# Decode attention on one core: the keys of a pair of units in one load, softmax parts of 160 and 96 tiles

## The chip, the cores and the metric

The kernel runs on one core of one Trainium2 chip. The metric is the device time of the execution in microseconds (us). A core has a TensorE (PE, matmul), a VectorE (DVE), a ScalarE (ACT), a GpSimd (POOL) and a SyncE (SP), and sixteen DMA engines that its queues share; SP's queue carries all loads of keys and values.

## The reference

Attention of one query position over 65,536 keys: 32 query heads of 128 elements, and 8 heads of keys and values, so that four query heads share one head of keys and values. All inputs are bfloat16.

```python
B, Hq, Hkv, Sq, Sk, D = 1, 32, 8, 1, 65536, 128

def reference(q, k, v):
    ...
    k = jnp.repeat(k, rep, axis=1)
    v = jnp.repeat(v, rep, axis=1)
    scale = D ** -0.5
    scores = jnp.einsum("bhqd,bhkd->bhqk", q, k) * scale
    p = _softmax(scores, axis=-1)
    return jnp.einsum("bhqk,bhkd->bhqd", p, v)
```

Keys and values are 134 MB each and are read once: 268.44 MB in all.

## The kernel before

**Work.** A head's 65,536 keys are four *units* of 16,384 (`HU = 4`); a unit is 128 *tiles* (`T`) of 128 keys. Two units of a head are a *pair*; there are 16 pairs (0 to 15), two for each head. In a pair, partition p holds 256 successive rows of keys (64 KB), and a tile is one row of each partition.

**Loads.** SP issues them in order. The keys of a pair come in two loads of 4 MB (128 partitions, 32 KB each) into `kbuf0` and `kbuf1`, one for each unit; the values of the pair come in one load of 8 MB (64 KB each partition) into `vbuf`. Before a key load SP waits for `kfree` of its buffer, before a value load for `vfree`. The first and the last loads are in pieces, so that work can start early and little is left behind the last one: the last unit's values come in pieces of 64, 32, 16, 10, 4 and 2 tiles (`V_PIECES`).

**One unit.** PE transposes tiles (by a matmul with the identity, line 125) in 16 groups of eight, into one of four PSUM banks `trb`; DVE (line 209) copies three of four groups to `ktb` in SBUF, ACT (line 207) the fourth (`on_act`). Then PE multiplies each transposed tile by the four queries `qcur` (line 136) into `qkb` of the unit, three groups (`LAG`) behind the transposes. When all scores of a unit are there, DVE takes their maximum for each partition (line 236), POOL the maximum over partitions (line 389), DVE combines it with the running maximum and gives the negative to ACT (lines 243 to 248), and ACT computes `alpha`, by which earlier sums are scaled (line 348), and four exponentials, one for each query, with their sums (line 352). An evicted group 15 gives the key buffer free (`kfree`, in `evict`, as soon as its transposes are done).

**A pair.** PE runs the keys of both units, then the values of both (line 155, 128 matmuls each, accumulated in `pvb`). DVE adds them to `acc` (lines 263, 269, 271) and only then increments `vfree`. The loop on PE is over pairs; DVE's is over heads, with both pairs written out.

**Order on the engines.** Each engine runs its instructions in the order written. `dve_round` and `act_round` fix by hand where the softmax steps stand between evictions; a wait (`take`) holds everything behind it on its engine. `pe_last` replaces the last value stage: it consumes the pieces as they land, and then the last result is transposed, scaled and stored by SP (line 440).

Of the kernel before, what the change touches and what calls it, by code (L numbers as in the profile page):

```python
# [22 lines left out]

LOOP_SLOT = 176


def on_act(j):
    return j % 4 == 3
# [14 lines left out]
def bass_standalone__gqa_softmax__decode_kernel(nc, q, k, v, out):  # L43
# [5 lines left out]
    assert D == P and Sk == P * T * HU and T * R == 512 and H >= 3 and NU % 2 == 0  # L49
# [27 lines left out]
    cmax = sb("cmax", [P, R], DT.float32)  # L77
# [5 lines left out]
    rsum = sb("rsum", [P, R], DT.float32)  # L83
# [12 lines left out]
    qkb = [S(nc.psum_tensor(f"qkb{i}", [P, T * R], DT.float32)) for i in range(2)]  # L96
    pvb = [S(nc.psum_tensor(f"pvb{i}", [P, 512], DT.float32)) for i in range(2)]
    fin = pvb[NU % 2]

    krdy = [sem(f"krdy{i}") for i in range(2)]  # L100
    khalf = [sem(f"khalf{i}") for i in range(2)]
    vrdy = [sem(f"vrdy{i}") for i in range(2)]
    vpiece = [sem(f"vpiece{i}") for i in range(len(V_PIECES))]
    kfree = [sem(f"kfree{i}") for i in range(2)]
    vfree = sem("vfree")
# [11 lines left out]
    def pe_transposes(pe, b, j):  # L117
        kv = kbuf[b][:, :].rearrange("p (t d) -> p t d", d=D)
        for i in range(TB):
            t = j * TB + i  # L120
            if t == 0:
                take(pe, krdy[b], 16)
            if t == HALF:
                take(pe, khalf[b], 16)
            ins = pe.transpose(trb[j % NTB][:, i * P:(i + 1) * P], kv[:, t, :], ident[:, :])  # L125
        ins.then_inc(tra if on_act(j) else trd, 1)

    def pe_scores(pe, b, j):
        done, (k, last) = eva if on_act(j) else evd, turn(j)
        if j == 0:  # L130
            take(pe, qrdy)
        if last:
            take(pe, done, k)
        for i in range(TB):
            t, off = j * TB + i, (j % NKG * TB + i) * P
            ins = pe.matmul(qkb[b][:, t * R:(t + 1) * R], lhsT=ktb[:, off:off + P],  # L136
                            rhs=qcur[:, :], start=True, stop=True)
            if i == 0 and not last:
                ins.wait_op(done, k, "sem-ge")
        if j == G - 1:  # L140
            ins.then_inc(qkd, 1)

    def pe_keys(pe, b):
        pend = []
        for j in range(G):
            pe_transposes(pe, b, j)
            pend.append(j)
            if len(pend) > LAG:
                pe_scores(pe, b, pend.pop(0))
        while pend:  # L150
            pe_scores(pe, b, pend.pop(0))

    def value(pe, b, t, first, last):
        vv = vbuf[:, :].rearrange("p (t d) -> p t d", d=D)
        return pe.matmul(pvb[b][:, 0:R], lhsT=vv[:, b * T + t, :], rhs=pts[b][:, t * R:(t + 1) * R],  # L155
                         start=t == first, stop=t == last)

    def pe_values(pe, b):
        take(pe, vrdy[b], 16)
        take(pe, exd)  # L160
        for t in range(T):
            ins = value(pe, b, t, 0, T - 1)
        ins.then_inc(pvd, 1)

    def pe_last(pe):
        b = (NU - 1) % 2
        starts = [sum(V_PIECES[:i]) for i in range(len(V_PIECES))]
        pe.wait_ge(t_o, H - 1)
        pe.transpose(qkb[0][0:HR - R, 0:P], oT[:, R:HR], identf[:, :]).then_inc(s_o, 1)
        take(pe, exd)  # L170
        for t in range(T):
            if t == starts[1]:
# [3 lines left out]
            ins = value(pe, b, t, 0, T - 1)  # L176
            if t in starts:
                ins.wait_op(vpiece[starts.index(t)], 16, "sem-ge")
# [5 lines left out]
    def tensor_engine(pe):  # L184
# [5 lines left out]
        with pe.Fori(0, NR) as i:  # L190
            pe_keys(pe, 0)
            pe_keys(pe, 1)
            pe_values(pe, 0)
            with pe.If(i < NR - 1):
                pe_values(pe, 1)
# [3 lines left out]
    def evict(e, n, j):  # L199
        dst = ktb[:, j % NKG * TB * P:(j % NKG + 1) * TB * P]  # L200
        k, last = turn(j)
        if last:
            take(e, tra if on_act(j) else trd, k)
        if j == G - 1:
            e.sem_inc(kfree[n % 2], 1)
# [4 lines left out]
        if not last:  # L210
            ins.wait_op(tra if on_act(j) else trd, k, "sem-ge")
# [10 lines left out]
    PART = [[j for j in range(a, b) if not on_act(j)] for a, b in ((0, 4), (4, 12), (12, G))]  # L222

    def evictions(e, n, parts):
        for part in parts:
            for j in part:
                evict(e, n, j)

    def scores_done(e, u):

        take(e, qkd)
        if u % HU == HU - 1:
            next_queries(e, qrdy)
        else:
            e.sem_inc(qrdy, 1)
        e.tensor_reduce(cmax[:, :], qkb[u % 2][:, :].rearrange("p (t g) -> p g t", g=R),  # L236
                        AX.X, ALU.max).then_inc(cm, 1)
# [12 lines left out]
    def add_sums(e, u):  # L250

        take(e, sx)
        if u % HU == 0:
            own(e, e.tensor_copy(lp[:, :], rsum[:, :]), xd)
        else:
            own(e, e.tensor_tensor(lp[:, :], lp[:, :], alpha[u % 2][:, :], ALU.mult), xd)  # L256
            own(e, e.tensor_tensor(lp[:, :], lp[:, :], rsum[:, :], ALU.add), xd)  # L257
# [7 lines left out]
    def add_values(e, u):  # L265
        take(e, pvd)
        pv = pvb[u % 2][:, 0:R]
        if u % HU == 0:
            own(e, e.tensor_copy(acc, pv), xd)  # L269
        else:  # L270
            own(e, e.tensor_tensor(acc, acc, pv, ALU.add), xd)  # L271

    def dve_round(e, i, h):

        a, b = 2 * i, 2 * i + 1
        evictions(e, a, PART)
        scores_done(e, a)
        evictions(e, b, PART[:1])
        maximum(e, a)
        evictions(e, b, PART[1:2])  # L280
        add_sums(e, a)
        evictions(e, b, PART[2:])
        scores_done(e, b)
        maximum(e, b)
        add_sums(e, b)
        rescale(e, a)
        add_values(e, a)
        rescale(e, b)
        if i < HALVES - 1:
            values_done(e, b)  # L290
        else:
            with e.If(h < H - 1):
                values_done(e, b)
                next_output(e)

    def values_done(e, u):
        add_values(e, u)
        e.sem_inc(vfree, 1)
# [23 lines left out]
    def vector_engine(e):  # L322
# [7 lines left out]
        with e.Fori(0, H) as h:  # L330
            for i in range(HALVES):
                dve_round(e, i, h)
        e.sem_inc(t_lp, 1)
        e.wait_ge(s_o, 1)
# [3 lines left out]
        ins = e.tensor_tensor(acc, acc, pvb[(NU - 1) % 2][:, 0:R], ALU.add)  # L338
# [6 lines left out]
    def exponentials(e, u):  # L345

        take(e, ng)
        e.activation(alpha[u % 2][:, :], dm[:, :], AF.Exp, scale=scale)  # L348
        sv = qkb[u % 2][:, :].rearrange("p (t g) -> p g t", g=R)
        pv = pts[u % 2][:, :].rearrange("p (t g) -> p g t", g=R)  # L350
        for g in range(R):
            ins = e.activation(pv[:, g, :], sv[:, g, :], AF.Exp, bias=negm[:, g:g + 1],  # L352
                               scale=scale, accum_out=rsum[:, g:g + 1])
# [4 lines left out]
    def act_round(e):  # L358
        for j in (3, 7, 11, 15):
            evict(e, 0, j)  # L360
        evict(e, 1, 3)
        exponentials(e, 0)
        for j in (7, 11, 15):
            evict(e, 1, j)
        exponentials(e, 1)

    def scalar_engine(e):
# [3 lines left out]
        with e.Fori(0, NR):  # L371
            act_round(e)
# [106 lines left out]
```

## Time and profile before

| | |
|---|---|
| median of 3 runs | 630.5 us (630.48 to 630.57) |
| the profiled execution | 630.56 us, span 628.5 us |
| PE busy | 489.2 us (78%) |
| DVE busy | 312.5 us (50%) |
| ACT busy | 186.6 us (30%) |
| POOL busy | 16.4 us (3%) |
| HBM read | 268.44 MB, 427 GB/s over the span |
| mean granted TensorE clock | 0.79 |

The span runs from the first to the last instruction of the profiled execution. PE's busy time is that of pipelined matmuls; PEld is its weight load, which overlaps. Rows of a timeline give the start and the duration in us, the engine, the line of the kernel and the operation. DMA rows of SP are issues; the transfer itself lands later.

### The profile page before, as it was taken

Reading aid. Unit: us, or ns where it says so; the run is one execution under the profiler, and the core shown is the slowest. Engines: PE = TensorE matmul, PEld = TensorE weight load, DVE = VectorE, ACT = ScalarE, POOL = GpSimd, SP = SyncE. Lnnn points to the kernel's source line nnn. Section 1 sums busy time; section 2 is a strip of 40 time slices with the busy share of each in tenths; the row PEclk is TensorE's granted clock in tenths of the full one; section 3 lists DMA queues with packets and bytes.
Section 4 is the critical chain, followed back from the end, with each engine's and each line's share of the span. In section 5 each row is a group of like instructions: output and inputs, shape, how many; then the busy total and the mean of one; then the engine's idle time right before and its main releaser. Section 6 shows DMA issues by size and latency. Waiting matters only on the chain. (4 is left out here: it accounts for less than half of the span.)

```text
span 628.5 us, 27046 instructions
## 1 busy us (share of the span) xinstructions
PE 489.2 (78%) x12293; PEld 482.3 (77%) x12293; DVE 312.5 (50%) x693; ACT 186.6 (30%) x418; POOL 16.4 (3%) x50
## 2 busy tenths in 40 slices
PE   4868859788696877967779686895868949689897
PEld 4758859687696877967679686895868949689896
DVE  4534726447273462725627256371563716537373
ACT  2321413314142141422414224041241413414141
POOL 0000000000000000000000000000000000000000
PEclk9776958769597695967959689696886969869596
DMA  8999999999999999999999999999999999999996
GB/s 369 439 426 446 434 415 453 415 453 430 419 448 419 448 419 434 453 413 455 407 432 438 425 438 430 430 455 409 455 413 438 442 415 448 417 434 432 423 444 283
DMA packets 8458, 268.58 MB, mean 427 GB/s; under 512 B 1026, under 2 KB 1282, under 8 KB 1538
## 3 DMA queue, kind: packets, MB, share of 16 engines
q1 hardware_dynamic: 8360, 268.44, 99.2%
q8 instruction: 7, 0.11, 0.1%
q10 hardware_dynamic: 90, 0.02, 0.0%
q14 instruction: 1, 0.01, 0.0%
HBM read 268.44 MB, written 0.01 MB: 427 GB/s over the span
## 5 line engine op out<-in xcount | busy, mean ns | idle before, releaser
L125 PE MATMUL trb<-ident,kbuf 128*128 128x128 bf16 x4096 | 328.3, 233 | 42.7 <-PEq L40 42.7
L209 DVE COPY ktb<-trb 128x1024 bf16<-128x1024 bf16 x384 | 254.2, 689 | 100.8 <-PE trb L125 97.5
L125 PEld LDWEIGHTS trb<-ident,kbuf 128*128 128x128 bf16 x4096 | 262.8, 105 | 43.7 <-issue 43.7
L207 ACT ACTIVATE ktb<-trb 128x1024 bf16<-128x1024 bf16 x128 | 131.1, 1024 | 379.1 <-PE trb L125 320.0
L136 PE MATMUL qkb<-qcur,ktb 128*128 128x4 bf16 x4096 | 170.9, 165 | 21.9 <-PEq L40 21.9
L136 PEld LDWEIGHTS qkb<-qcur,ktb 128*128 128x128 bf16 x4096 | 153.3, 97 | 26.0 <-issue 23.9
L155 PE MATMUL pvb<-pts,vbuf 128*128 128x4 bf16 x4096 | 112.3, 166 | 68.7 <-PEq L40 57.9
L155 PEld LDWEIGHTS pvb<-pts,vbuf 128*128 128x128 bf16 x4096 | 111.1, 104 | 70.1 <-issue 68.5
L352 ACT ACTIVATE pts<-qkb,negm 128x128 bf16<-128x128 f32 x128 | 50.5, 540 | 0.0
L236 DVE TENSOR_REDUCE cmax<-qkb 128x4 f32<-128x512 f32 x32 | 22.1, 692 | 43.2 <-DVEq L40 42.0
L271 DVE TENSOR_TENSOR acc<-acc,pvb 128x4 f32<-128x4 f32 x23 | 3.6, 158 | 62.8 <-DVEq L40 62.8
L352 ACT ACTIVATION_READ_ACCUMULATOR pts<-qkb,negm 128x1 f32 x128 | 34.6, 270 | 0.0
L389 POOL PARTITION_ALL_REDUCE cmaxa<-cmax x32 | 11.9, 372 | 576.3 <-POOLq L40 576.3
L348 ACT ACTIVATE alpha<-dm 128x4 f32<-128x4 f32 x32 | 6.6, 205 | 54.2 <-ACTq L40 53.4
L256 DVE TENSOR_TENSOR lp<-lp,alpha 128x4 f32<-128x4 f32 x24 | 3.8, 160 | 34.2 <-DVEq L40 34.2
L269 DVE COPY acc<-pvb 128x4 f32<-128x4 f32 x8 | 1.3, 162 | 25.5 <-DVEq L40 25.5
L246 DVE TENSOR_TENSOR m<-m,cmaxa 128x4 f32<-128x4 f32 x24 | 3.8, 159 | 11.5 <-DVEq L40 11.5
L218 DVE COPY qcur<-qT 128x4 bf16<-128x4 bf16 x9 | 1.5, 169 | 13.4 <-DVEq L40 13.3
L263 DVE TENSOR_TENSOR acc<-acc,alpha 128x4 f32<-128x4 f32 x24 | 3.9, 163 | 4.3 <-DVEq L40 1.9
L247 DVE TENSOR_TENSOR dm<-m 128x4 f32<-128x4 f32 x24 | 3.9, 162 | 3.5
L257 DVE TENSOR_TENSOR lp<-lp,rsum 128x4 f32<-128x4 f32 x24 | 3.9, 162 | 3.5
L391 POOL PARTITION_ALL_REDUCE la<-lp x8 | 3.4, 431 | 29.3 <-POOLq L40 29.3
(42 smaller groups left out, 23.7 us busy)
## 6 DMA issues: line engine op xcount, KB each, us to landing
kbuf<-in_k_dram SPq DMA_DIRECT2D x29, 4096.0 KB, 26.0
kbuf<-in_k_dram SPq DMA_DIRECT2D x6, 2048.0 KB, 21.1
vbuf<-in_v_dram SPq DMA_DIRECT2D x3, 4096.0 KB, 24.9
vbuf<-in_v_dram SPq DMA_DIRECT2D x1, 2048.0 KB, 29.4
vbuf<-in_v_dram SPq DMA_DIRECT2D x1, 1024.0 KB, 31.4
vbuf<-in_v_dram SPq DMA_DIRECT2D x1, 512.0 KB, 32.2
vbuf<-in_v_dram SPq DMA_DIRECT2D x1, 320.0 KB, 32.5
vbuf<-in_v_dram SPq DMA_DIRECT2D x14, 30.9
```

Of the source, the lines that this page charges most:

```text
L125: ins = pe.transpose(trb[j % NTB][:, i * P:(i + 1) * P], kv[:, t, :], ident[:, :])
L136: ins = pe.matmul(qkb[b][:, t * R:(t + 1) * R], lhsT=ktb[:, off:off + P], rhs=qcur[:, :], start=True, stop=True)
L155: return pe.matmul(pvb[b][:, 0:R], lhsT=vv[:, b * T + t, :], rhs=pts[b][:, t * R:(t + 1) * R], start=t == first, stop=t == last)
L207: ins = e.activation(dst, trb[j % NTB][:, :], AF.Copy).then_inc(eva, 1)
L209: ins = e.tensor_copy(dst, trb[j % NTB][:, :]).then_inc(evd, 1)
L236: e.tensor_reduce(cmax[:, :], qkb[u % 2][:, :].rearrange("p (t g) -> p g t", g=R), AX.X, ALU.max).then_inc(cm, 1)
L247: e.tensor_tensor(dm[:, :], mo[:, :], mn[:, :], ALU.subtract)
L257: own(e, e.tensor_tensor(lp[:, :], lp[:, :], rsum[:, :], ALU.add), xd)
L263: own(e, e.tensor_tensor(acc, acc, alpha[u % 2][:, :], ALU.mult), xd)
L348: e.activation(alpha[u % 2][:, :], dm[:, :], AF.Exp, scale=scale)
L352: ins = e.activation(pv[:, g, :], sv[:, g, :], AF.Exp, bias=negm[:, g:g + 1], scale=scale, accum_out=rsum[:, g:g + 1])
L389: e.partition_all_reduce(cmaxa[:, :], cmax[:, :], P, bass.bass_isa.ReduceOp.max).then_inc(cma, 1)
```

## The change

The keys of a pair are one load of 8 MB, with 64 KB for each partition, as the values are. `kbuf` is one buffer of 352 tiles: an even pair lies in tiles 96 to 351, an odd one in 0 to 255. Every pair's first 160 tiles (20 groups, `A`, `GA`) lie in tiles 96 to 255 of the buffer; the other 96 (`C`) lie behind them in an even pair and ahead of them in an odd one (`row_tile` maps a position to the row). So the next pair's keys may be loaded once group 19 is transposed. PE's code has the last 96 transposes twice, in two `If` blocks, for the two places.

The softmax runs over parts of 160 and 96 tiles. The first part's scores fill one PSUM bank and a quarter of a second, so it has two reductions and eight exponentials; the second part has one and four. PE scores the first 160 tiles three groups behind their transposes, then transposes all of the last 96, then scores these. DVE copies 23 of the 32 groups of a pair, ACT nine (24 and eight before); ACT's copies all stand ahead of its exponentials.

PE's value stage takes 64 tiles after the first part, 192 after the second, into three places of one bank. `vfree` is incremented when these matmuls are done, ahead of the additions. The last pair but one has keys and values in two loads each; the last has keys in three, and values in two and then pieces of 48, 24, 12, 6, 4 and 2 tiles.

Of the functions, the diff shows the lines of the new kernel, added and kept; the removed ones stand in the functions above.

```diff
@@ -9,23 +9,28 @@
 AX = mybir.AxisListType
 P = 128
 T = 128
+C = 96
+A = 2 * T - C
+K_PARTS = (0, 64, A)
 TB = 8
-G = T // TB
+G = 2 * T // TB
+GA = A // TB
+BANK = 512
 NTB = 4
-NKG = 8
+NKG = C // TB
 LAG = 3
 HU = 4
-HALF = T // 2
-V_PIECES = (64, 32, 16, 10, 4, 2)
-LOOP_SLOT = 176
+V_PIECES = (48, 24, 12, 6, 4, 2)
+LOOP_SLOT = 0
 def on_act(j):
-    return j % 4 == 3
+    return j % 4 == 2 if j < GA else (j - GA) % 3 == 1
...
+    def row_tile(odd, x):
+        return (x + C) % (2 * T) if odd else x
...
         return S(nc.semaphore(name))
-    kbuf = [sb(f"kbuf{i}", [P, T * D], DT.bfloat16) for i in range(2)]
+    kbuf = sb("kbuf", [P, (2 * T + C) * D], DT.bfloat16)
     vbuf = sb("vbuf", [P, 2 * T * D], DT.bfloat16)
     ktb = sb("ktb", [P, NKG * TB * P], DT.bfloat16)
-    pts = [sb(f"pts{i}", [P, T * R], DT.bfloat16) for i in range(2)]
+    pts = sb("pts", [P, 2 * T * R], DT.bfloat16)
     qsb = sb("qsb", [HR, D], DT.bfloat16)
     qT = sb("qT", [P, HR], DT.bfloat16)
...
@@ -114,68 +125,89 @@
+    def pe_transposes(pe, j, first):
+        for n, x in enumerate(K_PARTS):
+            if j == (x // TB if x < A else GA - 1):
+                take(pe, krdy[n], 16)
         for i in range(TB):
+            t = first + i
+            ins = pe.transpose(trb[j % NTB][:, i * P:(i + 1) * P], kbuf[:, t * D:(t + 1) * D],
+                               ident[:, :])
+            if i == 0 and j >= GA + NTB:
+                ins.wait_op(eva if on_act(j - NTB) else evd, turn(j - NTB)[0], "sem-ge")
         ins.then_inc(tra if on_act(j) else trd, 1)
+    def scores(x):
+        b = 2 if x >= A else x // T
+        return qkb[b], x - (0, T, A)[b]
+    def pe_scores(pe, j):
         done, (k, last) = eva if on_act(j) else evd, turn(j)
         if j == 0:
             take(pe, qrdy)
         if last:
             take(pe, done, k)
         for i in range(TB):
+            (bank, t), off = scores(j * TB + i), (j % NKG * TB + i) * P
+            ins = pe.matmul(bank[:, t * R:(t + 1) * R], lhsT=ktb[:, off:off + P],
                             rhs=qcur[:, :], start=True, stop=True)
             if i == 0 and not last:
                 ins.wait_op(done, k, "sem-ge")
+        if j in (T // TB - 1, GA - 1, G - 1):
             ins.then_inc(qkd, 1)
...
+    def pe_keys(pe, i):
+        for j in range(GA + LAG):
+            if j < GA:
+                pe_transposes(pe, j, C + j * TB)
+            if j >= LAG:
+                pe_scores(pe, j - LAG)
+        with pe.If(i % 2 < 1):
+            for j in range(GA, G):
+                pe_transposes(pe, j, C + j * TB)
+        with pe.If(i % 2 > 0):
+            for j in range(GA, G):
+                pe_transposes(pe, j, j * TB - A)
+        for j in range(GA, G):
+            pe_scores(pe, j)
+    def value(pe, out, r, first, last):
+        return pe.matmul(out, lhsT=vbuf[:, r * D:(r + 1) * D], rhs=pts[:, r * R:(r + 1) * R],
+                         start=first, stop=last)
+    def pe_values(pe):
+        for q, (a, b) in ((1, (C, A)), (0, (0, C)), (2, (A, 2 * T))):
+            if q in (1, 2):
+                take(pe, vrdy[q - 1], 16)
+            if q in (1, 0):
+                take(pe, exd)
+            for r in range(a, b):
+                ins = value(pe, pvb[:, q * R:(q + 1) * R], r, r == a, r == b - 1)
+        ins.then_inc(pvd, 1)
...
+    def pe_last(pe):
+        starts = [sum(V_PIECES[:i]) for i in range(len(V_PIECES))]
         take(pe, exd)
         pe.wait_ge(t_o, H - 1)
         pe.transpose(qkb[0][0:HR - R, 0:P], oT[:, R:HR], identf[:, :]).then_inc(s_o, 1)
+        for x in range(A):
+            ins = value(pe, pvb[:, 0:R], row_tile(True, x), x == 0, x == A - 1)
+            if x in (0, C):
+                ins.wait_op(vrdy[x // C], 16, "sem-ge")
+        ins.then_inc(pvd, 1)
         take(pe, exd)
+        for r in range(C):
+            if r == starts[1]:
                 pe.wait_ge(t_lp, 1)
                 pe.matmul(fin[0:R, P:P + 1], lhsT=lp[:, :], rhs=ones[:, :],
                           start=True, stop=True).then_inc(s_l, 1)
+            ins = value(pe, pvl[:, 0:R], r, r == 0, r == C - 1)
+            if r in starts:
+                ins.wait_op(vpiece[starts.index(r)], 16, "sem-ge")
         ins.then_inc(pvd, 1)
         ins = pe.transpose(fin[0:R, 0:P], acc, identf[:, :])
         ins.wait_op(t_acc, 1, "sem-ge")
...
+    def evict(e, j):
         dst = ktb[:, j % NKG * TB * P:(j % NKG + 1) * TB * P]
+        (k, last), done = turn(j), tra if on_act(j) else trd
         if last:
+            take(e, done, k)
+        if j == GA - 1:
+            e.wait_ge(done, k)
+            e.sem_inc(kfree, 1)
         if on_act(j):
             ins = e.activation(dst, trb[j % NTB][:, :], AF.Copy).then_inc(eva, 1)
         else:
             ins = e.tensor_copy(dst, trb[j % NTB][:, :]).then_inc(evd, 1)
+        if not last and j != GA - 1:
+            ins.wait_op(done, k, "sem-ge")
...
+    def evictions(e, a, b):
+        for j in range(a, b):
+            if not on_act(j):
+                evict(e, j)
+    def largest(e, b, n, to):
         take(e, qkd)
+        return e.tensor_reduce(to[:, :], qkb[b][:, 0:n * R].rearrange("p (t g) -> p g t", g=R),
+                               AX.X, ALU.max)
+    def first_part_done(e):
+        largest(e, 0, T, cmax[0])
+        own(e, largest(e, 1, A - T, cmax[1]), xd)
+        e.tensor_tensor(cmax[0][:, :], cmax[0][:, :], cmax[1][:, :], ALU.max).then_inc(cm, 1)
+    def pair_done(e, i):
+        if i == HALVES - 1:
             next_queries(e, qrdy)
         else:
             e.sem_inc(qrdy, 1)
...
+    def add(e, pv):
+        own(e, e.tensor_tensor(acc, acc, pv, ALU.add), xd)
+    def add_values(e, i):
+        rescale(e, 2 * i)
         take(e, pvd)
+        e.sem_inc(vfree, 1)
+        for n, q in enumerate((1, 2, 0) if i else (0, 1, 2)):
+            pv = pvb[:, q * R:(q + 1) * R]
+            if n == 2:
+                rescale(e, 2 * i + 1)
+            if i == 0 and n == 0:
+                own(e, e.tensor_copy(acc, pv), xd)
+            else:
+                add(e, pv)
...
     def dve_round(e, i, h):
         a, b = 2 * i, 2 * i + 1
+        evictions(e, 0, GA)
+        first_part_done(e)
+        evictions(e, GA, G - NTB)
         maximum(e, a)
+        evictions(e, G - NTB, G)
         add_sums(e, a)
+        largest(e, 2, C, cmax[0]).then_inc(cm, 1)
+        pair_done(e, i)
         maximum(e, b)
         add_sums(e, b)
         if i < HALVES - 1:
+            add_values(e, i)
         else:
             with e.If(h < H - 1):
+                add_values(e, i)
                 next_output(e)
...
@@ -344,32 +389,36 @@
     def exponentials(e, u):
         take(e, ng)
         e.activation(alpha[u % 2][:, :], dm[:, :], AF.Exp, scale=scale)
+        pv = pts[:, :].rearrange("p (t g) -> p g t", g=R)
+        for x, n, sums in ((A, C, 0),) if u % 2 else ((0, T, 0), (T, A - T, 1)):
+            bank, t = scores(x)
+            sv = bank[:, :].rearrange("p (t g) -> p g t", g=R)
+            r = row_tile(u // 2, x)
+            for g in range(R):
+                ins = e.activation(pv[:, g, r:r + n], sv[:, g, t:t + n], AF.Exp,
+                                   bias=negm[:, g:g + 1], scale=scale,
+                                   accum_out=rsum[sums][:, g:g + 1])
         own(e, ins, xa)
         e.sem_inc(exd, 1)
         e.sem_inc(sx, 1)
+    def act_round(e, i):
+        for j in range(G):
+            if on_act(j):
+                evict(e, j)
+        exponentials(e, 2 * i)
+        exponentials(e, 2 * i + 1)
...
     def sync_engine(e):
+        kp, vp = pairs(kf), pairs(vf)
+        def cols(a, b):
+            return slice(a * D, b * D)
+        def load_k(i, odd, split=(0,)):
+            for n, f in enumerate(split):
+                last = (split + (len(K_PARTS),))[n + 1]
+                a, b = K_PARTS[f], (K_PARTS + (2 * T,))[last]
+                r = row_tile(odd, a) if b - a < 2 * T else 0
+                t = r if odd else C + r
+                e.dma_start(kbuf[:, cols(t, t + b - a)], kp[i][:, cols(r, r + b - a)]).then_inc(krdy[f], 16)
+                for x in range(f + 1, last):
+                    e.sem_inc(krdy[x], 16)
+        def load_v(i, ready, a, b):
+            e.dma_start(vbuf[:, cols(a, b)], vp[i][:, cols(a, b)]).then_inc(ready, 16)
+        def load_both(i, odd):
+            take(e, kfree)
+            load_k(i, odd)
+            take(e, vfree)
+            load_v(i, vrdy[0], 0, 2 * T)
             e.sem_inc(vrdy[1], 16)
+        load_k(0, 0, (0, 1, 2))
+        load_v(0, vrdy[0], 0, 2 * T)
+        e.sem_inc(vrdy[1], 16)
+        load_both(1, 1)
+        with e.Fori(1, H - 1) as h:
+            load_both(2 * h, 0)
+            load_both(2 * h + 1, 1)
         i = NR - 2
+        take(e, kfree)
+        load_k(i, 0, (0, 2))
         take(e, vfree)
+        load_v(i, vrdy[0], 0, A)
+        load_v(i, vrdy[1], A, 2 * T)
         i = NR - 1
+        take(e, kfree)
+        load_k(i, 1, (0, 1, 2))
         take(e, vfree)
+        load_v(i, vrdy[0], C, 2 * C)
+        load_v(i, vrdy[1], 2 * C, 2 * T)
+        r = 0
+        for n, sm in zip(V_PIECES, vpiece):
+            load_v(i, sm, r, r + n)
+            r += n
         ins = e.dma_start(of[HR - R:HR, :], olast[:, :])
         ins.wait_op(t_last, 1, "sem-ge")
         ins.then_inc(o_sem, 16)
```

More of the change, by code (lines that the diff above doesn't have):

```diff
@@ L76, in bass_standalone__gqa_softmax__decode_kernel @@
     ones = sb("ones", [P, 1], DT.float32)
-    cmax = sb("cmax", [P, R], DT.float32)
+    cmax = [sb(f"cmax{i}", [P, R], DT.float32) for i in range(2)]
     cmaxa = sb("cmaxa", [P, R], DT.float32)
@@ L139, in pe_scores @@
                 ins.wait_op(done, k, "sem-ge")
-        if j == G - 1:
+        if j in (T // TB - 1, GA - 1, G - 1):
             ins.then_inc(qkd, 1)
[L143 to L156, printed above, removed]
@@ L332, in vector_engine @@
                 dve_round(e, i, h)
+        rescale(e, NU - 2)
+        take(e, pvd)
+        add(e, pvb[:, 0:R])
         e.sem_inc(t_lp, 1)
+        rescale(e, NU - 1)
         e.wait_ge(s_o, 1)
@@ L337, in vector_engine @@
         own(e, e.reciprocal(rl[:, :], fin[0:R, P:P + 1]), xd)
[L338 removed]
+        ins = e.tensor_tensor(acc, acc, pvl[:, 0:R], ALU.add)
         ins.wait_op(pvd, 1, "sem-ge")
@@ L370, in scalar_engine @@
         e.activation(dscr[:, 1:2], dscr[:, 0:1], AF.Exp, scale=1.0)
-        with e.Fori(0, NR):
-            act_round(e)
+        with e.Fori(0, H):
+            for i in range(HALVES):
+                act_round(e, i)
         e.wait_ge(t_row, 1)
```

135 lines of the change are left out of this document (15 added, 120 removed).

## The prediction

> **What bounds the kernel now.** I read the page first: the busy tenths of the DMA engines in 40 slices, the DMA queues and the issues.
>
> ```profile
> span 628.5 us, 27046 instructions
> DMA  8999999999999999999999999999999999999996
> q1 hardware_dynamic: 8360, 268.44, 99.2%
> q8 instruction: 7, 0.11, 0.1%
> qsb<-in_q_dram ACTq DMA_DIRECT2D x1, 8.0 KB, 2.2
> ```
>
> The load queue takes 99.2% of sixteen engines' span, and no slice between the first and the last is under nine tenths. So the kernel is bound by its loads, end to end. Then the DMA queue's own timeline, for one steady pair, and the landing times that go with it (the middle one of fourteen value loads; the two key loads of 491.63):
>
> ```profile
> 477.85 0.33 SPq L417 DMA_DIRECT2D vbuf<-in_v_dram  x1
> 491.63 11.61 SPq L413 DMA_DIRECT2D kbuf<-in_k_dram  x2
> 516.63 0.33 SPq L417 DMA_DIRECT2D vbuf<-in_v_dram  x1
> vbuf<-in_v_dram SPq DMA_DIRECT2D x14, 30.9
> DMA to landing us min/median/max: 25.3/26.1/26.9
> ```
>
> The value loads are issued 516.63 - 477.85 = 38.78 us apart: this is the period of a pair (8 MB of keys, 8 MB of values). Values land at 477.85 + 30.9 = 508.75; the second key load, issued at 491.63 + 11.61 - 0.33 = 502.91, lands 25.3 later, at 528.2; the next values at 547.5. So the key pair takes 19.45 and the values 19.3 (each to 0.1), and every load is issued long before the queue reaches it.
>
> The end is the third view, the chain in order of time, with the sizes and landings of the last pieces:
>
> ```profile
> 590.83 0.33 SPq L438
> ...
> 591.20 0.43 SPq L403
> ...
> 591.67 0.43 SPq L403
> ...
> 592.15 0.43 SPq L403
> ...
> 592.62 32.54 DMA vbuf<-in_v_dram
> ...
> 625.21 0.75 PE pvb L155 x16
> vbuf<-in_v_dram SPq DMA_DIRECT2D x3, 4096.0 KB, 24.9
> vbuf<-in_v_dram SPq DMA_DIRECT2D x1, 2048.0 KB, 29.4
> vbuf<-in_v_dram SPq DMA_DIRECT2D x1, 1024.0 KB, 31.4
> vbuf<-in_v_dram SPq DMA_DIRECT2D x1, 512.0 KB, 32.2
> vbuf<-in_v_dram SPq DMA_DIRECT2D x1, 64.0 KB, 32.1
> ```
>
> The last piece is issued at 593.57 (two steps of 0.475 after 592.62) and lands at 625.7; the last value matmul ends at 625.21 + 0.75 = 625.96, and 628.5 - 625.96 = 2.54 us of fixed tail follow. The profiled execution took 630.56 us, 2.06 more than its span; the median of the runs is 630.5, so I count from 630.5 and treat changes of the span as changes of the time.
>
> **Part 1, keys in one load.** The pieces price a load of 128 rows. 2 MB land at 591.20 + 29.4 = 620.6, the 1 MB after it at 623.07, the 0.5 MB at 624.35; the 4 MB before land at 590.83 + 24.9 = 615.73. Steps 4.87, 2.47, 1.28: halving the size leaves 2 x 2.47 - 4.87 = 0.07 and 2 x 1.28 - 2.47 = 0.09 us that don't halve. So each load costs some 0.08 us beside its bytes. Thirteen of the pairs 0 to 15 (1 to 13) go from two key loads to one; the last pair's keys from four to three and its values from seven to eight. Saved: 13 x 0.08 = 1.0 us. The bounds are nothing, and 13 x 0.15 = 2.0 by the 19.45 against 19.3 above; I take 1.0, from the pieces, whose steps are the cleaner. It lies on the path as long as the queue never runs dry and the loads still end last. By that the time would be 629.5.
>
> **Part 2, does the queue run dry?** Now keys of a pair arrive as a whole, so PE starts about 10 us later relative to the stream, and both buffers come free later. I build the new pair from the last pair of before, which starts right after a value stage as the new one's last pairs do:
>
> ```profile
> 591.45 3.57 PE L125 MATMUL trb<-ident,kbuf 128*128 128x128 bf16 x32 [1.17 <-PEq L40]
> 594.81 0.40 PE L136 MATMUL qkb<-qcur,ktb 128*128 128x4 bf16 x8
> 601.39 2.10 DVE L209 COPY ktb<-trb 128x1024 bf16<-128x1024 bf16 x3 [0.60 <-PE trb L125]
> 602.04 0.61 PE L125 MATMUL trb<-ident,kbuf 128*128 128x128 bf16 x8
> 602.68 0.61 PE L125 MATMUL trb<-ident,kbuf 128*128 128x128 bf16 x8
> 603.13 0.84 PE L136 MATMUL qkb<-qcur,ktb 128*128 128x4 bf16 x24
> 603.48 1.02 ACT L207 ACTIVATE ktb<-trb 128x1024 bf16<-128x1024 bf16 x1 [1.72 <-ACTq L40]
> 604.65 0.34 PE L136 MATMUL qkb<-qcur,ktb 128*128 128x4 bf16 x8 [0.68 <-PEq L40]
> 604.85 1.95 PE L125 MATMUL trb<-ident,kbuf 128*128 128x128 bf16 x32
> 606.64 0.34 PE L136 MATMUL qkb<-qcur,ktb 128*128 128x4 bf16 x8
> ```
>
> From the first transpose, s: sixteen groups of eight are transposed by 603.13 - 591.45 = 11.7; four more at 602.68 - 602.04 = 0.64 end at 14.3, and with that the new kfree is due (DVE group 19 waits for the transposes only). Draining the scores takes 604.99 - 603.13 = 1.86 in before, behind an ACT eviction of 1.02; now a DVE copy of 0.70 stands there: 1.54, so the first 160 tiles are scored at 15.8. The other twelve groups are transposed at (606.64 - 604.85) / 4 = 0.45 each: 21.2. DVE puts the two reductions between (below) and then eight copies of 0.70, about 22.5 at the end, just beside PE; I charge nothing, and up to 1 us if it is late. Their 96 scores at 0.84 / 3 = 0.28 for eight: 24.6.
>
> The softmax, from a steady pair:
>
> ```profile
> 78.63 0.69 DVE L236 TENSOR_REDUCE cmax<-qkb 128x4 f32<-128x512 f32 x1
> 80.71 0.20 ACT L348 ACTIVATE alpha<-dm 128x4 f32<-128x4 f32 x1 [3.43 <-ACTq L40]
> 82.12 0.28 ACT L352 ACTIVATION_READ_ACCUMULATOR pts<-qkb,negm 128x1 f32 x1
> 82.52 6.97 PE L155 MATMUL pvb<-pts,vbuf 128*128 128x4 bf16 x256 [4.75 <-ACTq L355]
> 82.73 0.16 DVE L256 TENSOR_TENSOR lp<-lp,alpha 128x4 f32<-128x4 f32 x1 [2.13 <-DVEq L40]
> 83.04 0.16 DVE L257 TENSOR_TENSOR lp<-lp,rsum 128x4 f32<-128x4 f32 x1
> 90.09 0.33 SPq L417 DMA_DIRECT2D vbuf<-in_v_dram  x1
> ```
>
> ACT now queues all nine evictions ahead of the first part's exponentials; its last copy starts near 20.9 and ends at 21.9. Four exponentials of 128 tiles take 82.40 - 80.71 = 1.69 from alpha, four of 32 tiles (no row has them; between the read alone, 0.27, and the full step, 0.34) 1.1 more: first part done at 24.8. DVE is held at its wait for these sums, and behind that wait stands the second part's reduction: two sums at 0.31 for a head's first pair, three otherwise: 25.4. From reduction to alpha 2.08, less a quarter of 0.5 for 96 tiles: 1.95, 27.4; from alpha to the first value matmul 82.52 - 80.71 = 1.81, less 0.16: 29.0. Of the values 64 tiles are done before that; the other 192 at 6.97 / 256 = 0.0272 take 5.2: **34.3 us for a pair, 34.6 for a head's second**. The value buffer is announced 0.3 after that (0.6 in before, with an addition of 0.31 that now comes later).
>
> So in the steady state keys are issued at s + 14.5 against 19.3 when the queue is through with the values, and values at s + 34.9 against 38.8. A small load takes 2.2 from issue to landing (qsb above), an upper bound for the pick-up: 2.6 and 1.7 us are left. The queue stays fed; this cover is thin, and once gone each us costs 13.
>
> **Part 3, the end.** The cover hides the late start only while loads follow. Let T be the landing of pair 13's keys: 528.2 - 1.0 = 527.2. Loads go on as in before: their last piece lands at 625.7 - 1.0 = 624.7, T + 97.5. PE is a chain from T: pair 13 starts at T + 0.1 and ends at 34.7; pair 14's first 160 tiles have landed 7.3 (3 of 8 MB) before the whole, at T + 31.5, so it starts at once and ends at 69.0; pair 15 likewise (its first 160 tiles land at T + 70.3 in two pieces, the first 64 at 63.1). There the first part is done at 69.0 + 24.8 = 93.8; one transpose of an output (estimated at 0.34, as eight scores above) and 160 values (4.4) end at 98.5, just after the second part is ready at 69.0 + 29.3 = 98.3; 96 values take 2.6: **T + 101.1**, with every value piece long landed. The fixed tail of 2.54 makes the span 527.2 + 101.1 + 2.5 = 630.8, against 628.5: plus 2.3, thus **632.8**. The loads alone would let the values end at T + 97.8. So the end is no longer a transfer: 3.3 us of PE, DVE and ACT stand behind it, more than twice what the loads gain.
>
> The sum is least sure of the start of a pair: the first four groups take 594.81 - 591.45 = 3.36, 0.84 each, and later ones alone 0.45. If the slow clock holds two groups more or fewer in each of three pairs, that is 0.8 x 3 = 2.4 either way; exponentials at 0.34 and a late DVE add up to 1. The forecast's own range is 630.4 to 636.
>
> **Rivals.** *The loads still end last: 629.5.* This needs 3.3 us less over three pairs, 1.1 each, for instance all groups at the full clock (16 groups in 9.5 instead of 11.7). For it speaks that my waits are upper sums of handoffs; against it that the first 3.36 us were slow after a value stage in the very row used. 14%.
>
> *Code is fetched in each pair.* Two branches now skip or end a block of 96 transposes inside PE's loop, which grows from 768 to 864 matmuls as it stands in memory. If each needed a fetch, the nearest row is the idle of 1.17 before 591.45 (which also waits for a landing): 2.4 a pair, three pairs at the end 7.2, and the value load's cover of 1.7 is overrun by 0.7 x 13 = 9: 640 to 649. Against: seven instruction packets in the whole run, while PE took its loop's backward branch fifteen times. 5%. [...]
>
> *The last 96 tiles run at the slow clock*: 12 x (0.84 - 0.45) = 4.7 more a pair, the value load would come 3 us late in thirteen pairs, 39, and the end 14: 686. PE is busy throughout that stretch, so 3%. [...]
>
> *64 KB rows are no quicker but slower*, so the change doesn't do what it says:
>
> ```profile
> 43.40:62.80 19.40, 16.72 (x442) 16.63 (x443) 6.61 (x13) 2.77 (x3) 0.00 (x0) 0.65 1.03 443
> 62.90:82.20 19.30, 13.50 (x328) 13.07 (x325) 12.20 (x28) 8.50 (x24) 0.74 (x2) 0.97 0.97 421
> ```
>
> By windows the stretch in which keys land moves 443 GB/s and the next, of values, 421. Taken at its word this costs 19.4 x 22 / 421 = 1.0 a pair, 13 in all: 647. But both stretches move 8 MB in 19.4 and 19.3 us; a packet is booked whole in one window, and packets in flight at the border shift the sum. 3%.
>
> **How the numbers follow.** The forecast has 75%, the four rivals 14, 5, 3 and 3. A measurement of this kernel can tell about 0.2% (1.26 us) from no change. Faster by more than that (under 629.2) is the first rival with a larger saving of loads: 6%. Within it lie the rest of that rival, 8, and the forecast's low end up to 631.8, some 14: 22%. Slower: 72%. The range goes from 629.3, which takes in the first rival, to 636.5; the three dear rivals and the edges, under 2 in 10, are left out.
>
> **What would show it.** Right: value issues 38.70 apart; q1 near 98.7% of a span of 630.8 (622.5 us of packets); key issues some 14.5 and value issues some 35 us after a pair's first transpose; the last chain no longer a transfer but PE, ACT and DVE back over pairs 14 and 15, with the last piece landed 3 us before the last value matmul. Wrong: the chain ends in a value transfer again (then the first rival, or my handoffs are too long); value issues over 39 apart (a dry queue); gaps of over 1 us in PE at the inner branches; transposes of the last 96 tiles over 0.1 us apart.

## The result and the profile after

The changed kernel takes 641.2 us (median of 5 runs, 637.7 to 641.7) against 630.5 (630.5 to 630.7): ratio 1.0155, 95% interval 1.0127 to 1.0183. It is slower, as forecast, but by 10.7 us where 2.3 were forecast, and outside the range. The profiled execution took 641.53 us.

The page of the profile after: the span, the DMA engines in 40 slices, the load queue, the instruction queue, and the chain that ended last.

```profile
span 639.7 us, 27108 instructions
DMA  9999999999999999999999999999999999999994
q1 hardware_dynamic: 6488, 268.44, 98.2%
q8 instruction: 9, 0.15, 0.1%
PE qkb L178 0%; PE pvb L212 0%; DVE olast L386 0%; PE pvb L206 0%; DVE acc L383 0%; DVEq L377 0%
```

The chain no longer ends in a transfer; that was forecast. But the queue's packets now fill 0.982 x 639.7 = 628.2 us, 5.7 more than the 622.5 forecast: the "busy" tenths stay at 9 while the queue loses time. The queue's own timeline (each row an issue by SP) shows it, with the time to landing of the issues at 77.28, 97.90, 116.82, 136.86, 155.83 and 176.45 below it, in this order:

```profile
77.28 0.34 SPq L459 DMA_DIRECT2D kbuf<-in_k_dram  x1
97.90 0.34 SPq L464 DMA_DIRECT2D vbuf<-in_v_dram  x1
116.82 0.33 SPq L459 DMA_DIRECT2D kbuf<-in_k_dram  x1
136.86 0.33 SPq L464 DMA_DIRECT2D vbuf<-in_v_dram  x1
155.83 0.33 SPq L459 DMA_DIRECT2D kbuf<-in_k_dram  x1
176.45 0.33 SPq L464 DMA_DIRECT2D vbuf<-in_v_dram  x1
...
DMA to landing us min/median/max: 24.3/24.3/24.3
DMA to landing us min/median/max: 24.2/24.2/24.2
DMA to landing us min/median/max: 24.7/24.7/24.7
DMA to landing us min/median/max: 24.0/24.0/24.0
DMA to landing us min/median/max: 24.4/24.4/24.4
DMA to landing us min/median/max: 23.8/23.8/23.8
```

The landings are at 101.6, 122.1, 141.5, 160.9, 180.2 and 200.3. So the loads take 20.5 (values), 19.4 (keys), 19.4 (values), 19.3 (keys) and 20.0 (values). A load that is not late takes 19.35 here; the 8 MB value loads of before take 19.34 to 19.36. The values of 97.90 were issued 3.7 us ahead of the landing of the load in front and lost 1.2; those of 136.86, with 4.6, lost nothing; those of 176.45, with 3.8, lost 0.65. Roughly every second value load loses: the time that one loses is the next one's head start, here 4.6 after 3.7. By the completion times that the trace keeps, seven value loads lose 7.4 us and all others together 0.8. The last piece lands at 632.86 (at 625.69 before): saved 1.0, lost 8.2.

One pair from its first transpose (101.74) to the announcement of its values (136.86), rows of PE and DVE:

```profile
101.74 1.54 PE L136 MATMUL trb<-ident,kbuf 128*128 128x128 bf16 x13 [4.15 <-PEq L45]
...
117.66 5.53 PE L136 MATMUL trb<-ident,kbuf 128*128 128x128 bf16 x96
...
127.53 0.56 DVE L260 TENSOR_REDUCE cmax<-qkb 128x4 f32<-128x384 f32 x1 [0.26 <-DVEq L45]
...
131.29 5.26 PE L178 MATMUL pvb<-pts,vbuf 128*128 128x4 bf16 x192 [2.78 <-PEq L45]
```

Counted from 101.74: first 160 tiles scored at 15.9 (forecast 15.8), second reduction at 25.8 (25.4), last 192 values at 29.55 (29.0), their end at 34.8 (34.3), value issue at 35.1 (34.9). The chain is as forecast within 0.5 us.

The end, PE's rows, and the row of the last piece (issued at 607.00):

```profile
619.69 5.53 PE L136 MATMUL trb<-ident,kbuf 128*128 128x128 bf16 x96 [0.17 <-issue]
...
628.87 4.40 PE L178 MATMUL pvb<-pts,vbuf 128*128 128x4 bf16 x160
633.64 1.42 PE L178 MATMUL qkb<-pts,vbuf 128*128 128x4 bf16 x48 [0.38 <-PEq L45]
...
635.70 1.44 PE L178 MATMUL qkb<-pts,vbuf 128*128 128x4 bf16 x48
...
vbuf<-in_v_dram SPq DMA_DIRECT2D x1, 64.0 KB, 25.9
```

The last piece lands at 632.9 and the last value matmul ends at 637.14. In before it ended 0.3 after the landing, so 4.0 us of PE's work stand behind the loads; 3.3 were forecast.

### The profile page after: what moved, and what is told of

Same layout as the page of the kernel before. It is cut to its first block, busy times and chain, and to the rows that moved or that the text cites. A ratio compares the mean times of both kernels' runs of the same rounds, so it can differ in the third digit from the quotient of the medians.

```text
span 639.7 us, 27108 instructions
## 1 busy us (share of the span) xinstructions
PE 484.3 (76%) x12293; PEld 477.2 (75%) x12293; DVE 311.0 (49%) x740; ACT 214.7 (34%) x562; POOL 16.4 (3%) x50
## 5 line engine op out<-in xcount | busy, mean ns | idle before, releaser
L136 PE MATMUL trb<-ident,kbuf 128*128 128x128 bf16 x4096 | 304.2, 232 | 73.0 <-PEq L45 71.6
L136 PEld LDWEIGHTS trb<-ident,kbuf 128*128 128x128 bf16 x4096 | 258.5, 104 | 74.7 <-issue 74.6
L240 DVE COPY ktb<-trb 128x1024 bf16<-128x1024 bf16 x368 | 243.5, 689 | 126.8 <-PE trb L136 122.9
L238 ACT ACTIVATE ktb<-trb 128x1024 bf16<-128x1024 bf16 x144 | 147.5, 1024 | 362.7 <-PE trb L136 356.2
L155 PE MATMUL qkb<-qcur,ktb 128*128 128x4 bf16 x4096 | 149.4, 165 | 8.9 <-issue 5.3
L155 PEld LDWEIGHTS qkb<-qcur,ktb 128*128 128x128 bf16 x4096 | 136.8, 97 | 12.0 <-issue 5.4
L401 ACT ACTIVATE pts<-qkb,negm 128x128 bf16<-128x128 f32 (+2 forms) x192 | 63.3, 460 | 0.0
L401 ACT ACTIVATION_READ_ACCUMULATOR pts<-qkb,negm 128x1 f32 x192 | 48.1, 255 | 0.0
L260 DVE TENSOR_REDUCE cmax<-qkb 128x4 f32<-128x512 f32 (+2 forms) x48 | 23.9, 510 | 7.9 <-DVEq L45 7.9
L305 DVE TENSOR_TENSOR acc<-acc,pvb 128x4 f32<-128x4 f32 x38 | 6.0, 157 | 36.0 <-DVEq L45 31.6
```

Source lines behind the costliest of these rows:

```text
L136: ins = pe.transpose(trb[j % NTB][:, i * P:(i + 1) * P], kbuf[:, t * D:(t + 1) * D], ident[:, :])
L155: ins = pe.matmul(bank[:, t * R:(t + 1) * R], lhsT=ktb[:, off:off + P], rhs=qcur[:, :], start=True, stop=True)
L238: ins = e.activation(dst, trb[j % NTB][:, :], AF.Copy).then_inc(eva, 1)
L240: ins = e.tensor_copy(dst, trb[j % NTB][:, :]).then_inc(evd, 1)
L260: return e.tensor_reduce(to[:, :], qkb[b][:, 0:n * R].rearrange("p (t g) -> p g t", g=R), AX.X, ALU.max)
L401: ins = e.activation(pv[:, g, r:r + n], sv[:, g, t:t + n], AF.Exp, bias=negm[:, g:g + 1], scale=scale, accum_out=rsum[sums][:, g:g + 1])
```

## The experiments

In all of them the kernel before took 630.5 to 630.6 (medians). The trace keeps 16 signals of each load, and I take each for the end of one of the sixteen DMA engines; the landing is the last of them. "Lead to the first engine" is from the issue of a load to the first of the 16 signals of the load in front, "lead to the landing" from the issue to the last.

**Sums behind the second maximum (e1).**

```diff
-        add_sums(e, a)
         largest(e, 2, C, cmax[0]).then_inc(cm, 1)
+        add_sums(e, a)
```

> The changed kernel with the second part's reduction ahead of the sums of the first part on DVE (one line moved). In its trace the reduction starts 1.7 us after its scores are done, because the sums wait for ACT; a pair should take 33.5 us instead of 34.8. Theory (the value load of every even pair is issued too late, 3.7 us before the keys ahead of it have landed, and the engines run dry): the late landings, 0.7 to 1.7 us in every second pair, 8 us in all, go, and the end of the chain over pairs 13 to 15 comes 3 to 4 us sooner: 629.5 to 631.5. Rival (64 KB key rows or the inner branches cost time in each pair, whatever the lead of the issue): only the end moves, by 4: 637.

Measured 638.7 (632.9 to 641.2), ratio 1.0108 (1.0067 to 1.0149): over both expected times, so the late landings did not go. In the profiled run the last piece lands at 631.08. The values are announced earlier, but now keys are late too: the key loads issued at 156.64 and 235.25 lead the first engine by 2.2 and 2.0 us and take 20.6 and 20.0. Nor does the lead to the landing, with which I had reckoned (about 5 us), order the loads: late in this run a key load with 4.2 us to the landing lost nothing; the engines then ended only 1.0 us apart, and it led the first one by 3.25.

**The kernel before, values announced late (e2):** POOL runs 14 or 18 small reductions between the additions and `vfree`.

> The kernel before, with the value buffer announced later: POOL takes DVE's signal, runs 14 (first pair of a head) or 18 (second) small reductions on a scratch tile, about 6.3 or 8.1 us, and then frees the buffer. Nothing else waits for these. Value loads are then issued about 5.3 and 3.5 us before the keys ahead of them have landed, instead of 11.6. Theory (a load of 8 MB needs about 5 us from issue until all sixteen engines move it at full rate): none or 0.2 us lost at 5.3, 1 to 1.7 at 3.5, seven times: 637 to 642. Rival (2.2 us are enough, as the prediction assumed, and the loss in the changed kernel comes from its key rows or its code): 630.5 as before.

Measured 641.6 (two runs), ratio 1.0175 (1.0155 to 1.0196). Its SP rows, and the time to landing of the values of 101.60, 139.44 and 180.50, then of the second key load of each x2 row (issued at 115.73 and 156.46):

```profile
101.60 0.33 SPq L430 DMA_DIRECT2D vbuf<-in_v_dram  x1
104.44 11.62 SPq L426 DMA_DIRECT2D kbuf<-in_k_dram  x2
139.44 0.33 SPq L430 DMA_DIRECT2D vbuf<-in_v_dram  x1
144.96 11.83 SPq L426 DMA_DIRECT2D kbuf<-in_k_dram  x2
180.50 0.33 SPq L430 DMA_DIRECT2D vbuf<-in_v_dram  x1
...
DMA to landing us min/median/max: 21.8/21.8/21.8
DMA to landing us min/median/max: 22.8/22.8/22.8
DMA to landing us min/median/max: 21.9/21.9/21.9
DMA to landing us min/median/max: 27.1/27.1/27.1
DMA to landing us min/median/max: 25.2/25.2/25.2
```

The keys in front land at 142.8 and 181.6. The delays came out longer than planned: leads of 3.4 and 1.1 to the landing, not 5.3 and 3.5. With 1.1 a load takes 20.7, with 3.4 it takes 19.35. That the time lies in the expected range is therefore luck, and the 5 us of that theory fall. But the rival (2.2 us are enough, and the loss comes from key rows or code) expected no loss: the old kernel, with its 32 KB key rows and its short code, loses in the same way once it announces late. The engines there end 0.5 us apart, and 3.4 to the landing (2.9 to the first one) is enough.

**Each value load in two (e3):** 160 and 96 tiles instead of 256.

> The changed kernel with each value load in two, of 160 and 96 tiles, issued one after the other at the same time as the one was. Theory: the issue is as late as before, so the late landings stay, and fourteen more loads cost 0.08 us each: 642. Rival (the pick-up is slow because of the 64 KB rows or the size of the load): the first load is picked up sooner, the losses of 8 us shrink to half or less: 637.

Measured 640.8 (638.6 to 642.4): as the changed kernel. In its profiled run, of 639.15, the last piece lands at 631.43, 5.7 us later than in before, which has as many loads. The size of the value load is not the cause.

**Keys of pair 13 in two loads (e4):** 160 and 96 tiles, so that PE gets its head start two pairs earlier.

> The changed kernel with the keys of pair 13 in two loads, 160 and 96 tiles, as pair 14 has them. PE can then start pair 13 as soon as pair 12's values are done, some 4 us before its keys have all landed, and the whole chain behind it to the end moves by that. Theory (the last 4.0 us of the changed kernel are PE, DVE and ACT behind the last landing): 637.2, and the last chain nears a transfer. Rival (the end has the loads behind it, the loss is all in the steady pairs): 641 as it was.

Measured 638.7 (636.3 to 640.1), 2.5 less than the changed kernel where 4 were expected; the runs of the two overlap. The loads of the profiled run still end at 632.58; what it wins is the tail, 5.7 from there to the span's end instead of 6.9. PE came 2.3 us earlier to its last values and then stood still for 1.85 within them (below).

**Keys of every pair in two loads (e6).**

```diff
-            load_k(i, odd)
+            load_k(i, odd, (0, 2))
```

> The changed kernel with the keys of every pair from the second on in two loads, 160 and 96 tiles, into the same buffer; nothing else moves. Theory (a load is lost when it is issued less than about 3 us before the FIRST of the 16 engines has finished the load ahead; the engines finish about 2 us apart): transposes start with the landing of the first 160 tiles, some 7.3 us earlier than with one load (a 96-tile load takes 7.30), so every announcement leads by some 7 us more and no load is late; the loads end at 632.86 - 8.2 (lost) + 13 x 0.07 (12.12 + 7.30 against 19.35) = 625.6. The span then ends 5.75 us after the last landing, not 2.8 as before the change, because TensorE's code for the last 107 value matmuls arrives only as the queue of loads runs dry (it resumed 0.1 us around the last landing in the three runs so far): span 631.3, time 633.2, range 632.3 to 634.2. Rival 1 (announcements are the whole of it, the tail as before the change): 630.3. Rival 2 (the 64 KB rows, the alternating offsets or the longer code of TensorE cost time by themselves): 638 or more, with loads still over 19.42 in places that have a lead.

Measured 633.2 (632.0 to 633.6), ratio 1.0035 (1.0023 to 1.0046): as the theory said. Three windows from 60 to 580 us, first of before, then of the changed kernel, then of this one; the last column is GB/s:

```profile
60.00:580.00 520.00, 408.58 (x10349) 403.64 (x10347) 263.64 (x573) 157.78 (x353) 13.06 (x34) 0.79 1.00 433
```

```profile
60.00:580.00 520.00, 402.65 (x10191) 397.42 (x10192) 258.08 (x601) 176.31 (x458) 12.69 (x33) 0.76 1.00 427
```

```profile
60.00:580.00 520.00, 408.83 (x10335) 403.58 (x10333) 263.95 (x611) 179.66 (x462) 13.04 (x34) 0.77 1.00 433
```

6 GB/s over 520 us are 3.1 MB, 7.2 us at 433 GB/s: by this coarse measure (1 GB/s is 1.2 us) most of the 8.2 lost, and it is gone. From 90 us on value issues have leads of over 8 us to the first engine and every 256-tile load takes 19.35; the last piece lands at 625.84 (expected 625.6). Offsets, parts, 64 KB value rows and the longer code of PE are as in the changed kernel, so none of them costs the queue anything.

**Leads by other means (e7):** the edit of e1, and the scores 8 groups behind the transposes (`LAG = 8`; each transpose waits for its PSUM bank); all loads as large as in the changed kernel.

> The changed kernel with two edits that only bring announcements forward, and every load as large as in it: VectorE takes the second part's maximum ahead of the sums, which made the pair 1.3 us shorter, and the scores follow the transposes by 8 groups, not 3 (every transpose waits for its PSUM buffer), so that the 160th tile is transposed, and the keys announced, about 1 us earlier. Theory (lead to the first engine of about 3 us is enough): both kinds of load lead the first engine by about 3 us, lose 0 to 0.15 each, the loads end near 626, and the end comes 5.75 us behind that and 1.85 for the rest: 633.6, range 632.5 to 635. Rival (64 KB rows or the offsets cost time by themselves, or the engines' unequal ends cost it at any lead): as the kernel with the maximum ahead alone, 638 to 639.

Measured 635.4 (634.3 to 637.2); the profiled run, of 634.25, lies in the range, the median 0.4 above it. In that run, from 100 us on, nearly all loads of 64 KB rows lead the first engine by 2.8 to 4.4 and take 19.35, and the last piece lands at 625.58. Two of its value issues, eight pairs apart, with their time to landing, and the window of 60 to 580 us:

```profile
213.20 0.33 SPq L464 DMA_DIRECT2D vbuf<-in_v_dram  x1
...
521.68 0.33 SPq L464 DMA_DIRECT2D vbuf<-in_v_dram  x1
...
DMA to landing us min/median/max: 24.5/24.5/24.5
DMA to landing us min/median/max: 25.7/25.7/25.7
...
60.00:580.00 520.00, 406.96 (x10341) 404.30 (x10342) 263.19 (x610) 179.05 (x461) 13.03 (x34) 0.77 1.00 432
```

The values land at 237.7 and 547.4: 38.71 us a pair, where before took 38.78 and 38.70 were forecast. So one key load for a pair does save what Part 1 says, as long as it is announced in time.

Over the changed kernel, e1, e3 and e4 together, by lead to the first engine (rounded to 0.5; from the completion times, loads from 60 us on, mean over the 16 engines):

| lead to the first engine, us | 1.5 | 2.0 | 2.5 | 3.0 | 3.5 | 4.0 |
|---|---|---|---|---|---|---|
| loads | 6 | 23 | 25 | 21 | 12 | 12 |
| lost by a load, us | 0.79 | 0.55 | 0.28 | 0.05 | 0.04 | 0.00 |

**The standstill in the last values (e9, e12).** PE's last rows in e6:

```profile
620.00 4.09 PE L178 MATMUL pvb<-pts,vbuf 128*128 128x4 bf16 x149
625.98 0.43 PE L178 MATMUL pvb<-pts,vbuf 128*128 128x4 bf16 x11 [1.89 <-issue]
...
627.75 1.44 PE L178 MATMUL qkb<-pts,vbuf 128*128 128x4 bf16 x48
```

PE waits for nothing that its rows show, and the span ends 6.0 us behind the last landing. First I put 72 waits that are already met ahead of PE's loop (e9):

> As the kernel with every pair's keys in two loads, and 72 waits that are already met on TensorE ahead of its loop, which move its code by 72 instructions against the 16 KB blocks in which it is fetched. [...] Now the loop's end lies 72 instructions later, so that the loop itself enters the block that holds the first value matmuls behind it, and the next one is fetched 570 us earlier; the next border lies at about matmul 241 of 256, so that nothing large waits: the end comes about 2.8 us after the last landing, at 630.4 (629.9 to 631.2). Rival 1 (what is fetched ahead is fixed, and the border only moves from matmul 149 to 113): the stall holds 143 matmuls, 0.9 to 1 us more than the kernel without the waits, about 634.2. Rival 2 (the stall is no code fetch): as the kernel without them, within 0.3.

Measured 632.1 (631.8 to 633.6), the runs of e6 and of this one overlap; the standstill stays at matmul 149 with 2.03 us. When a block of code is fetched, and that the next border lies at about matmul 241, on both of which the 630.4 rests, no run shows; here the standstill stayed where it was. PE went on at 624.20 here, ahead of the last landing at 625.6, so it doesn't wait for the loads to run out either. Then the same waits behind the loop (e12):

> Every pair's keys in two loads, and 72 waits that are already met behind TensorE's loop and ahead of its last values; two of them go into one instruction, so they are 36 instructions and some 2 us. If the standstill in the last values is a block of code that comes late, its border moves by 36 instructions, 18 matmuls: the standstill is then at matmul 131, not 149. If it hangs on the operands (a semaphore, a value piece, a bank), it stays at 149. Time: 2 us over the kernel without the waits by the first, 635, or less if the block has more time to come.

Measured 634.2, one run:

```profile
620.82 3.68 PE L178 MATMUL pvb<-pts,vbuf 128*128 128x4 bf16 x131
626.08 0.91 PE L178 MATMUL pvb<-pts,vbuf 128*128 128x4 bf16 x29 [1.59 <-issue]
```

36 more instructions (27,168 on its page, 27,132 on that of e6), and the standstill moves by 18 matmuls of two instructions (weight load and matmul): it hangs on a place in PE's code, which I take for a border between blocks of it. The instruction queue, too, points to late code: in e6 it has a packet of 16 KB from 623.5 to 624.7, and PE goes on 1.3 behind its end. In all eight runs with a standstill PE goes on 1.3 to 1.5 behind the end of such a packet; in the changed kernel and in e7, where it ended 1.4 before PE reached matmul 149, there is no standstill. Why code ahead of the loop doesn't move it (the kernels align the loop's start) was not tried.

**All together (e10, e11).** e10 has the edits of e7, pair 13 split and the waits ahead of the loop; e11 the edits of e7 and every pair split.

> The two edits that bring announcements forward (maximum ahead of the sums, scores 8 groups behind), the keys of pair 13 in two loads, and the 72 waits ahead of TensorE's loop. If the leads and the code block are all that the changed kernel loses: loads end near 626, the end 2.8 us behind: 630.6, range 629.8 to 631.5, which is the kernel before. If the waits only move the border of the block: 634.5. If the 64 KB rows cost time by themselves: 637 or more.

> Every pair's keys in two loads, and the two edits that bring announcements forward (maximum ahead of the sums, scores 8 groups behind): the kernel in which no load can be late and TensorE is earliest at the end. With the keys in two loads alone the loads ended at 625.84, and behind them stood TensorE: its last values began at 620.0, stood still for 1.89 us at matmul 149, and ended at 629.44. Theory: the loads end at 625.8 as there, the values begin 2 to 3 us earlier (1.3 from the maximum, 1 from the scores), the standstill stays, 6 us behind their beginning, and the last matmuls end near 627: 630.8, range 630.2 to 632. Rival 1 (TensorE's lead at the end is set by the last value landings of the pair before, so that the chain doesn't matter): 633.2 as with two loads alone. Rival 2 (the standstill goes when TensorE is earlier): 629.5 or less, under the kernel before.

e10: 632.2 (630.1 to 638.7), ratio 1.0053 (1.0019 to 1.0087), over its range; some runs reach the kernel before, others lose up to 8 us, and no trace of these was kept. e11: 631.6 (631.3 to 633.2), ratio 1.0023 (1.0013 to 1.0032), within its range. Its standstill stays (2.11 us); no load is late, and it is still no faster than before. No version found beats the kernel before.

## Why the prediction was right or wrong

**Part 1 was right.** Saved 1.0 us: the changed kernel's landings less what late loads lost, and 38.71 us a pair in e7 against 38.78.

**Part 2 failed, in one step.** The value load's head start came out nearly as worked out: 3.6 to 4.3 us to the landing of the load in front for the seven that lost most, 3.9 forecast. The step that failed is "an upper bound for the pick-up: 2.6 and 1.7 us are left": 2.2 us from a small load alone, and counted against the landing. A landing is the end of the last engine. The engines end 2.0 us apart in before (1.5 to 2.8 in the changed kernel's steady pairs), so the first one is free some 2 us sooner, and by the table it needs its next work about 3 us ahead: a 5 us head start to the landing where 2.2 were allowed. The cover of 1.7 was in truth short by over 1. The price was named ("once gone each us costs 13"), but not put into the sum, and about half of it came, 8.2 us: a load that has lost gives the next its head start, so only about every second value load loses.

**Part 3 was right in what ends last, and its size is in part luck.** 3.3 us of PE behind the loads, 4.0 measured, on loads that end 8.2 us later; 8.2 + 0.7 = 8.9 are the distance from the forecast span of 630.8 to 639.7. But from the landing of pair 13's keys (534.29) the last value matmul ends 102.85 later, not 101.1: 0.38 and 0.51 of this are waits within the last values, for their exponentials and for DVE's addition, which the sum put at nothing. The last piece lands 98.57 behind T, not 97.5, since two value loads there are late too, and this hides most of the error.

**The rivals.** The first (loads still end last) fell with the chain. Fetches in each pair: PE's idle at the inner branch is 0.17 us above, at most 0.22 in any pair, and the instruction queue has nine packets, not dozens. The slow clock in the last 96 tiles: 5.53 / 96 = 0.058 us each, at a granted clock of 1.00 from 117.66 to 123.20. (That PE is busy, the prediction's ground against this rival, doesn't settle it. Around the row of before that it used, the granted clock was 0.50 from 582.7 to 596.3, though PE was busy for 6.5 of the 8.7 us ahead of 591.4, at no time idle for more than 1.2, and busy throughout from 591.45 to 594.81. What brings the slow clock no run shows.) 64 KB rows slower: key loads of 64 KB rows take 19.35 as the values do. What happened was no rival of mine but stood among the signs of a wrong forecast: value issues over 39 us apart, 39.0 and 39.6 by the rows above, 39.3 on average from 97.90 to 529.87.

That a dry queue is the cause is shown from both sides: e2 makes the old kernel lose by it, e6 and e7 take the loss from the new one by different means. What sets the 2 us between engines, and the 3 us, stays open. The 3 us are an average: in e7 a load with a lead of 2.26 lost nothing, and in e2, where the engines end some 0.5 us apart, the late loads come to 1.35 lost + 0.6 of lead, only 2.0.

## What to carry to other kernels

Count the head start of a load against the first DMA engine that runs out, not against the landing of the load in front: subtract the spread of the engines' ends (some 2 us here), and leave beside it what a load needs (some 3 us here). When a change makes loads larger, buffers are freed later and in larger lumps (here the steady value loads lead the landing in front by 3.6 to 6.4 us, by 11.6 before); work out the announcement of each load against the queue before counting what the larger load saves. A queue that lost 0.6 us in a pair of 39 looked full in the busy tenths: compare GB/s over the steady stretch, or issue to landing.

## What the runs showed of the hardware

The ends of the sixteen engines lie apart and stay so: in e6 1.93 to 2.04 us over some 500 us; after running dry together (e2) they are 0.4 to 0.8 apart.

TensorE's straight code behind a loop stood still for 1.85 to 2.13 us in six kernels (e1, e4, e6, e9, e10, e11), 1.59 in e12 and 0.76 in e3, at a place that moved in e12 with the 36 instructions put in ahead of it (matmul 149 to 131) and stayed in e9. Each packet of the instruction queue q8 has 16,384 bytes, seven in before and nine in the changed kernel. The packet of code begins 3.5 to 3.7 us behind the first of the last value matmuls in those six, where the loads still go on for 5.8 us or more behind it, and 1.5 to 1.6 in the changed kernel and e7, where they go on for 4.0 and 3.3 and no standstill is seen (160 matmuls in 4.40 and 4.45 us). That fits code that comes late while the loads go on; no run tests it alone.
